# A linear-attention block and a gated spatial mixer in one program: denominators as one 1/den row per head, key weights loaded on ScalarE's queue, and a new order of all operations

## The chip, the cores and the metric

The program runs on one core of one Trainium2 chip. The metric is device time in microseconds (us) for one execution. A profile of one execution gives its span, from the first to the last instruction, and the trace that the later sections read.

## What is computed

Two blocks follow each other on x of 2048 tokens by 512 features (bf16). The first is a linear attention with 32 heads of 16 features, behind a layernorm and with a residual; the second is a gated mixer over the tokens, again behind a layernorm and with a residual. Cut to what matters:

```python
q, k, v = (layernorm(x) @ wqkv) split into 3 x 32 heads x 16
phi = lambda t: where(t > 0, t + 1, exp(t)) + 1e-06
pq, pk = phi(q), phi(k)
kv  = einsum('bhsd,bhse->bhde', pk, v)
z   = einsum('bhsd->bhd', pk)
num = einsum('bhqd,bhde->bhqe', pq, kv)
den = einsum('bhqd,bhd->bhq', pq, z)[..., None] + 1e-06
h   = x + (num / den) @ wo
zz  = gelu(layernorm(h) @ w_in);  z1, z2 = halves of 896 each
g   = w_sp @ layernorm(z2) + b_sp
h2  = h + (z1 * g) @ w_out
```

## The kernel before

**Stages.** The tokens are 16 tiles of 128 (NT) in 4 groups of 512 (NG, GW). In order of the data: layernorm of each x tile (DVE statistics, L571 and L575; 1/sqrt of the variance on ScalarE for tiles 0 to 3, on GpSimd for the others), transposition of the normalised tile (TensorE and a ScalarE copy, L640 and L647, for tiles 0 to 3; DMA transposes for the others), keys per tile (L729) and queries per group (L743), phi (Exp, Relu on ScalarE, L706 and L708, the rest on DVE), the product of pk with the normalised x (L761), the sum z (L773), a small chain that folds v and wo into one 512 x 512 matrix `mw` (L810, L828), the denominators (L843 to L874), attention plus residual (L893, L898), second layernorm, the two halves of the gelu layer (L925, L956), the mixing with `w_sp` (L995) and the last projection with its store (L1013, L1019, L1021).

**1/sqrt on ScalarE.** `rstd_act` (L584) is two activations on a 128 x 1 column: Ln of the variance (L585), then Exp of -1/2 times it (L587). Tiles 0 to 3 each have such a pair. ScalarE evaluates functions from a loaded table set. The kernel asks for one set by name, in a single operation of its own (L552), which no other operation is declared to depend on:

```python
op("act", 1.3, lambda e: e.preload_act_table_set("natural_log_exp_and_others"), bias=BIG - 1)
```

**Denominators before.** `den(gq)` works on one group of 512 tokens. Four matmuls (L843) multiply the columns `zb` (128 x 32 for each chunk c of 128 query features) with the queries; each writes its own 32 rows of one PSUM bank, so a row is a head of that chunk (eight heads, each repeated four times) and a column a token. ScalarE makes 1/den as exp(-ln(den)) on 128 x 512 (L848, L850). Four matmuls with 32 rows each (L858) spread the rows with the 0/1 matrix `sel` to the 128 feature rows of each chunk, into two tiles of two PSUM banks. One tile goes through a ScalarE copy to bf16 (L868) and a DVE product in SBUF (L870), the other straight into a DVE product with PSUM (L873). `den` is called once for each group.

**What sets the order.** `Program.op` only records operations with their reads and writes; from these come the semaphore waits. `Program.schedule` (L208) takes the order written out in `ORDER` (L15): a list of operation numbers, counted in the order in which the code records them. Each engine runs its own operations in that order, strictly one after the other. `SLOT` (L53) gives each temporary tile its PSUM bank or buffer. The costs and `LAG` are a planner's figures; no time on the chip follows from them.

On ScalarE the order before begins: the table load L552; Ln x0, Ln x1, Exp x0, Exp x1, Ln x2, Exp x2; the copies of transposed tiles 0, 1, 2; Ln x3, Exp x3; the copy of tile 3; then phi of the keys and of the queries of group 0. On SP it begins: loads of x tiles 0, 1, 2; the key weights `wk` (512 KB); x tile 3; the query weights `wq`; x tiles 4 to 15. On TensorE it begins: 8 matmuls on constants (L559), which give nothing to the result, three more of them behind DVE and ScalarE steps of tile 0, the transpositions of tiles 0, 1 and 2 with four short constant matmuls between and behind them, the keys of tiles 0 and 2, the transposition of tile 3, the keys of tile 1, and the first query chunk of group 0 (L743), which needs all four transposed tiles.

**The end.** The last tile is projected in two column ranges, 384 and 128 wide. Each is added to the residual by DVE and stored by a DMA that SP issues.

Of the kernel before, what the change touches and what calls it, by code (L numbers as in the profile page):

```python
# [5 lines left out]
FP32 = mybir.dt.float32  # L6
# [4 lines left out]
P = 128  # L11
# [48 lines left out]
]  # L60


# [1029 lines left out]
```

## Time and profile before

| | |
|---|---|
| median of 3 runs | 242.62 us (242.61 to 242.78) |
| span of the profiled execution | 241.1 us |
| TensorE busy | 236.2 us, 98% of the span |
| DVE busy | 135.3 us |
| ScalarE busy | 84.3 us |
| granted TensorE clock | 1.000 |

The profile gives the profiled execution's span; 1.5 us of the median (242.62 - 241.1) lie outside it. A row of the trace's timeline has the start in us, the busy us, the engine, the line, the operation, its output and input, how many instructions, and in brackets how long the engine had stood idle before and what ended that. PE is the matmul part of TensorE, PEld its weight loads, which run beside matmuls; ACT is ScalarE, POOL GpSimd, SP the engine whose queue issues most DMAs. A row of the chain of work that ended last has start, duration and the line, with the number of instructions.

### The profile page before, as it was taken

Reading aid. Unit: us, or ns where it says so; the run is one execution under the profiler, and the core shown is the slowest. Engines: PE = TensorE matmul, PEld = TensorE weight load, DVE = VectorE, ACT = ScalarE, POOL = GpSimd, SP = SyncE. Lnnn points to the kernel's source line nnn. Section 1 sums busy time; section 2 is a strip of 40 time slices with the busy share of each in tenths; the row PEclk is TensorE's granted clock in tenths of the full one; section 3 lists DMA queues with packets and bytes.
Section 4 is the critical chain, followed back from the end, with each engine's and each line's share of the span. In section 5 each row is a group of like instructions: output and inputs, shape, how many; then the busy total and the mean of one; then the engine's idle time right before and its main releaser. Section 6 shows DMA issues by size and latency. Waiting matters only on the chain.

```text
span 241.1 us, 2991 instructions
## 1 busy us (share of the span) xinstructions
PE 236.2 (98%) x1143; PEld 107.6 (45%) x1166; DVE 135.3 (56%) x269; ACT 84.3 (35%) x105; POOL 33.9 (14%) x87
## 2 busy tenths in 40 slices
PE   8999999999999999999999999999999999999995
PEld 2544443434444444445444444444444444444442
DVE  4899944699999986725833233342333423332443
ACT  4695744997776998455510000000000000000000
POOL 5123412002224472201300000000000000000000
PEclk9999999999999999999999999999999999999999
DMA  6933349954304343874544454430000100000022
GB/s 179 343 65 69 64 88 312 290 118 89 75 15 128 69 90 82 226 128 93 104 90 107 93 98 96 109 109 24 0 0 0 65 24 0 0 0 3 0 87 87
DMA packets 56702, 21.83 MB, mean 91 GB/s; under 512 B 50704, under 2 KB 55824, under 8 KB 56688
## 3 DMA queue, kind: packets, MB, share of 16 engines
q1 hardware_dynamic: 55744, 17.32, 32.4%
q0 software_dynamic: 944, 4.33, 5.3%
q8 instruction: 9, 0.15, 0.2%
q14 instruction: 5, 0.04, 0.1%
HBM read 7.47 MB, written 2.10 MB: 40 GB/s over the span
## 4 chain that ended last, share of the span: by engine, by line
PE 98%; issue 1%; DVEq 0%; DVE 0%
PE ps L995 40%; PE ps L925 10%; PE ps L956 10%; PE ps L1013 10%; PE ps L893 6%; PE ps L743 6%; PE ps L729 6%; PE ps L761 6%; PE ps L559 2%; PE ps L858 1%; PE ps L843 1%; PE ps L640 0%; PE ps L773 0%; PE ps L828 0%; PE ps L810 0%
## 5 line engine op out<-in xcount | busy, mean ns | idle before, releaser
L995 PE MATMUL ps<-wsp,pk_xn_z 128*128 128x512 bf16 x330 | 73.5, 379 | 0.3
L1002 DVE TENSOR_TENSOR e<-ps,e 128x512 bf16<-128x512 f32 x28 | 19.4, 692 | 64.0 <-PE ps L995 64.0
L995 PEld LDWEIGHTS ps<-wsp,pk_xn_z 128*128 128x128 bf16 x336 | 32.9, 98 | 39.4
L956 PE MATMUL ps<-hT,win 128*128 128x512 bf16 x110 | 26.4, 379 | 0.1
L925 PE MATMUL ps<-win,hT 128*128 128x384 bf16 (+1 forms) x124 | 26.0, 352 | 0.2
L1013 PE MATMUL ps<-wout,xT_pq_z 128*128 128x512 bf16 (+2 forms) x117 | 24.6, 366 | 0.1
L995 PE MATMUL ps<-wqkv_wsp,pk_xn_z 128*128 128x512 bf16 x109 | 24.2, 379 | 0.2
L934 DVE BATCH_NORM_STATS2 small<-pk_xn_z 128x6 f32<-128x512 bf16 (+1 forms) x32 | 18.4, 612 | 10.1 <-ACT pk_xn_z L930 10.0
L571 DVE BATCH_NORM_STATS2 small<-xh 128x6 f32<-128x512 bf16 x32 | 21.0, 675 | 3.3 <-DMA xh<-in_A_x_dram 3.2
L706 ACT ACTIVATE e<-ps 128x1024 bf16<-128x1024 f32 x16 | 16.5, 1032 | 9.7 <-PE ps L729 6.3
L961 ACT ACTIVATE xT_pq_z<-ps 128x1024 bf16<-128x1024 f32 (+1 forms) x16 | 14.5, 914 | 11.5 <-PE ps L956 11.5
L925 PEld LDWEIGHTS ps<-win,hT 128*128 128x128 bf16 x128 | 12.4, 98 | 12.6 <-issue 0.2
L1019 DVE TENSOR_TENSOR e<-ps,xh 128x512 bf16<-128x512 f32 (+2 forms) x17 | 11.1, 659 | 11.4 <-PE ps L1013 11.4
L1013 PEld LDWEIGHTS ps<-wout,xT_pq_z 128*128 128x128 bf16 x119 | 11.4, 98 | 13.1
L995 PEld LDWEIGHTS ps<-wqkv_wsp,pk_xn_z 128*128 128x128 bf16 x112 | 11.0, 98 | 13.2
L956 PEld LDWEIGHTS ps<-hT,win 128*128 128x128 bf16 x112 | 11.0, 98 | 12.6
L592 POOL TENSOR_TENSOR small<-small 128x2 f32<-128x2 f32 x22 | 16.4, 745 | 1.2
L930 ACT ACTIVATE pk_xn_z<-ps 128x896 bf16<-128x896 f32 x16 | 14.5, 914 | 5.3 <-PE ps L925 5.1
L743 PE MATMUL ps<-xT_pq_z,wqkv_wsp 128*128 128x512 bf16 x61 | 15.2, 380 | 0.3 <-issue 0.2
L729 PE MATMUL ps<-wqkv_wsp,xT_pq_z 128*128 128x512 bf16 x62 | 15.3, 379 | 0.1
L761 PE MATMUL ps<-pk_xn_z 128*128 128x512 bf16 x63 | 15.2, 379 | 0.2 <-issue 0.2
L590 POOL TENSOR_SCALAR small<-small 128x2 f32<-128x2 f32 x22 | 6.2, 280 | 63.2 <-DVE small L575 62.8
(72 smaller groups left out, 187.7 us busy)
## 6 DMA issues: line engine op xcount, KB each, us to landing
out_dram<-e SPq DMA_DIRECT2D x15, 128.0 KB, 1.7
win<-in_B_w_in_dram POOLq DMA_DIRECT2D x1, 1792.0 KB, 8.6
wqkv_wsp<-in_A_wqkv_dram SPq DMA_DIRECT2D x2, 512.0 KB, 4.5
xh<-in_A_x_dram SPq DMA_DIRECT2D x4, 256.0 KB, 5.5
wout<-in_B_w_out_dram POOLq DMA_DIRECT2D x1, 896.0 KB, 6.1
wsp<-in_B_w_sp_dram SPq DMA_TRANSPOSE x48, 2.9
xh<-in_A_x_dram SPq DMA_DIRECT2D x4, 128.0 KB, 2.5
xh<-in_A_x_dram SPq DMA_DIRECT2D x1, 512.0 KB, 6.8
```

The lines of the kernel that those rows point to most:

```text
L571: op("dve", dve_c(512), lambda e: e.bn_stats(s6.ap(), src.ap()), r=[src], w=[s6])
L592: return op("pool", 0.7, lambda e: e.tensor_tensor(dst.ap(), dst.ap(), h.ap(), ALU.pow), r=[dst, h], w=[dst])
L706: op("act", act_c(n), lambda e: e.activation(lo.ap(), t(flat).ap(), ACT.Exp), r=[t()], w=[lo])
L729: i = e.matmul(t(bank(ti)).ap(), lhsT=lhs.ap()[:, c, :], rhs=rhs.ap()[:, c, :], start=(c == 0), stop=(c == KD - 1))
L743: r_ = e.matmul(t(bank(i)).ap(), lhsT=lhs.ap()[:, c, :], rhs=rhs.ap()[:, c, :], start=(c == 0), stop=(c == KD - 1))
L761: r = e.matmul(txk[h](bank(i)).ap(), lhsT=xx.ap()[:, c * P:(c + 1) * P], rhs=kk.ap(), start=(n == 0), stop=(n == NT - 1))
L925: k = e.matmul(t(bank(i)).ap()[:, 0:b - a], lhsT=l.ap()[:, c, :], rhs=win[c, a:b].ap(), start=(c == 0), stop=(c == KD - 1))
L934: op("dve", dve_c(b - a), lambda e, s6=s6, src=src: e.bn_stats(s6.ap(), src.ap()), r=[src], w=[s6])
L956: k = e.matmul(t(bank(i)).ap(), lhsT=l.ap()[:, c, :], rhs=r_.ap()[:, c, :], start=(c == 0), stop=(c == KD - 1))
L995: k = e.matmul(t(bank(0)).ap(), lhsT=l.ap()[:, s - a, :], rhs=r_.ap()[:, s - a, :], start=(s == 0), stop=(s == NT - 1))
L1002: op("dve", dve_c(512), lambda e: e.tensor_tensor(gb().ap(), t(bank(0)).ap(), bsp().ap()[:, tg * GW:(tg + 1) * GW], ALU.add), r=[t(), bsp( ...
L1013: k = e.matmul(t(bank(0)).ap()[:, 0:b - a], lhsT=l.ap()[:, fc, :], rhs=wout[fc, a:b].ap(), start=(fc == 0), stop=(fc == KF - 1))
```

## The change

It has these parts.

1. **Denominators.** The query features are no longer taken in chunks of 128 neighbours but with a step of 4 (`f + i:D:KD`), so that each of the 32 heads has 4 rows in every chunk. The four chunks then add up in one row per head: `den(gs)` takes two groups of 512 tokens at once, with 16 matmuls of 128 x 32 by 256 columns that accumulate over c into four blocks of 32 rows, one block for each 128 tokens of a group. Ln and Exp are on 128 x 256, for two groups together. Four matmuls of 128 x 128 by 128 columns spread the rows of a group into one PSUM bank; ScalarE copies it to bf16 (128 x 512), and two DVE products in SBUF, each over half of the group's tokens with the row repeated for the four chunks, finish. `mw` is made by 16 matmuls of 32 output rows instead of 4 of 128.
2. **Loads.** `wk` is issued first on ScalarE's queue, beside SP's x0 to x3.
3. **Last tile.** The column ranges are 352 and 160; the second range's store is issued by ScalarE.
4. **Constant matmuls.** 9 at the start instead of 8; 3 later ones instead of 7.
5. **Order.** `ORDER` and `SLOT` are new for all operations. The planner's figures change too, without another effect.

```diff
 ORDER = [
-    29, 15, 0, 30, 18, 17, 21, 1, 16, 22, 31, 2, 13, 23, 32, 14, 3, 24, 33, 11, 4, 25, 34, 12, 5, 35, 38, 26, 6, 36,
...
+    27, 18, 21, 22, 28, 0, 13, 29, 30, 31, 32, 33, 34, 35, 24, 1, 15, 11, 12, 14, 36, 37, 38, 39, 2, 43, 44, 3, 4, 5,
...
+    86, 87, 106, 88, 143, 89, 148, 134, 97, 149, 90, 142, 83, 95, 91, 98, 150, 155, 156, 99, 26, 144, 104, 92, 100,
...
-    WARM = 8
+    WARM = 9
...
-    VIA_ACT = ((0, 0), (1, 0), (2, 0), (3, 0))
+    DEN = ((0, 1), (2, 3))
...
+    load("act", "wk", wqkv[:, D:2 * D], w3[:, :, D:2 * D], D * D * 2)
     load_x("sp", 0, 1)
     load_x("sp", 1, 2)
     load_x("sp", 2, 3)
-    load("sp", "wk", wqkv[:, D:2 * D], w3[:, :, D:2 * D], D * D * 2 + 50000)
     load_x("sp", 3, 4)
...
-    for gate, n, cost, count in ((first[0], 512, 2 * MM, 2), (rs_op[0], 512, 2 * MM, 1), (tr_op[0], 256, MM, 2),
-                                 (tr_op[1], 256, MM / 2, 2)):
+    for gate, n, cost, count in ((tr_op[0], 256, MM, 2), (tr_op[1], 256, MM / 2, 1)):
...
-            lhs = wqkv[:, (f + i) * P:(f + i + 1) * P]
+            lhs = wqkv[:, f + i:D:KD]
...
-                i = e.matmul(tzT(bank(0)).ap()[:, c * CG:(c + 1) * CG], lhsT=zr_v.ap[:, c * P:(c + 1) * P], rhs=part.ap,
+                i = e.matmul(tzT(bank(0)).ap()[:, c * CG:(c + 1) * CG], lhsT=zr_v.ap[:, c:D:KD], rhs=part.ap,
...
+        def mwmm(e, t=t, b=b):
+            for i in range(2):
+                for c in range(KD):
+                    k = e.matmul(t(bank(i)).ap()[CG * c:CG * (c + 1), :],
+                                 lhsT=kvT.ap()[:, c * P + 2 * b + i:(c + 1) * P:KD], rhs=wo[c, :].ap(),
+                                 start=True, stop=True, skip_group_check=True)
...
-    def den(gq):
+    def den(gs):
+        n = len(gs)
         t = Tile(PS)
-        r_ = pqT[gq].all()
+        pq = View(s_tq, (NG + gs[0]) * GB_, [n, KD, GW], BF16)
 
         def mm(e):
             for c in range(KD):
-                i = e.matmul(t(bank(0)).ap()[CG * c:CG * (c + 1), :], lhsT=zb.ap[:, CG * c:CG * (c + 1)],
-                             rhs=r_.ap()[:, c, :], start=True, stop=True)
+                for j in range(TPG):
+                    o = t(bank(0)).ap()[CG * j:CG * (j + 1), 0:n * P].rearrange("p (g k) -> p g k", g=n)
+                    i = e.matmul(o, lhsT=zb.ap[:, CG * c:CG * (c + 1)], rhs=pq.ap[:, :, c, j * P:(j + 1) * P],
+                                 start=(c == 0), stop=(c == KD - 1), skip_group_check=True)
             return i
...
+        op("act", act_c(n * P, 1), lambda e: e.activation(
+            flat(rr.ap()), t(bank(0)).ap()[:, 0:n * P], ACT.Ln, bias=eps[1:2].ap(), scale=1.0),
+           r=[t(), eps[1:2]], w=[rr])
+        last_lnexp.append(op("act", act_c(n * P), lambda e: e.activation(rb.ap(), rr.ap(), ACT.Exp, scale=-1.0),
+                             r=[rr], w=[rb]))
+        for gq in gs:
...
+                for j in range(TPG):
+                    k = e.matmul(t2(bank(0)).ap()[:, j * P:(j + 1) * P], lhsT=sel.ap[:, j * P:(j + 1) * P], rhs=r1.ap(),
+                                 start=True, stop=True, skip_group_check=True)
+                return k
+            op("pe", 4 * MS, sp_, r=[sel.all(), r1], w=[t2()])
+            op("act", act_c(GW), lambda e, t2=t2, rs=rs: e.activation(rs.ap(), t2(bank(0)).ap(), ACT.Copy), r=[t2()],
+               w=[rs])
+            for a in (0, GW // 2):
+                d, m = pqT[gq][:, a:a + GW // 2], rs_v[gq, a:a + GW // 2]
+                op("dve", dve_c(KD * GW // 2, 2), lambda e, d=d, m=m: e.tensor_tensor(
+                    d.ap(), d.ap(), m.ap().rearrange("p (a f) -> p a f", a=1).to_broadcast([P, KD, GW // 2]),
+                    ALU.mult), r=[d, m], w=[d])
...
-            op("sp", 0.5, lambda e, a=a, b=b, o_=o_: e.dma_start(out_dram[n * P:(n + 1) * P, a:b],
+            op("act" if a else "sp", 0.5, lambda e, a=a, b=b, o_=o_: e.dma_start(out_dram[n * P:(n + 1) * P, a:b],
...
-        project(n, [(0, D)] if n < NT - 1 else [(0, D - P), (D - P, D)])
+        project(n, [(0, D)] if n < NT - 1 else [(0, 352), (352, D)])
```

Counted through, the numbers of the new `ORDER` give these beginnings. The operation of L552 is number 26 (0 is the load of `wk`, 1 to 10 are SP's loads, 11 to 25 GpSimd's constants); ScalarE runs: the DMA of `wk`; Ln x0, Exp x0, Ln x1, Exp x1; copy of tile 0; Ln x2, Exp x2; copy of tile 1; Ln x3, Exp x3; copies of tiles 2 and 3; Exp of key pair 0; Exp, Relu of key pair 1; Exp, Relu of two query chunk pairs of group 0; Exp of key pair 2; **then number 26, the table load**; Exp of key pair 3 and so on. TensorE runs: 9 constant matmuls, transposition of tile 0, 2 constant ones, tile 1, 1 constant one, keys of tile 0, transposition of tile 2, keys of tile 1, transposition of tile 3, keys of tile 2, then the first query chunk of group 0. Further on, on TensorE, the denominators of groups 0 and 1 stand together in one place and those of groups 2 and 3 in another, and the two halves of the `mw` matmuls are neighbours. DVE's begin: statistics and aggregate of x0, of x1, normalisation of x0, statistics of x2, normalisation of x1, aggregate of x2, statistics of x3, normalisation of x2, aggregate of x3, statistics of x4, normalisation of x3.

More of the change, by code (lines that the diff above doesn't have):

```diff
@@ L154 @@
     __slots__ = ("eng", "fn", "cost", "prio", "deps", "after", "tiles", "seq", "start", "end", "pos", "sem",
-                 "semval", "marked", "clock", "lag", "bytes", "grp", "raw", "bias", "land", "late")
+                 "semval", "marked", "clock", "lag", "bytes", "grp", "raw", "bias", "land", "late", "mode")
 class Program:
     ENGINES = ("pe", "act", "dve", "pool", "sp")
-    LAG = {"pe": 0.17, "act": 0.12, "dve": 0.09, "pool": 0.1, "sp": 0.0}
+    LAG = {"pe": 0.163, "act": 0.1, "dve": 0.083, "pool": 0.045, "sp": 0.0}
     HOP = 0.06
@@ L170, in __init__, with op @@
         self.bias, self.late = 0.0, False
-    def op(self, eng, cost, fn, r=(), w=(), bias=0.0, after=(), dma=None, nbytes=0, land=2.0, lag=None):
+    def op(self, eng, cost, fn, r=(), w=(), bias=0.0, after=(), dma=None, nbytes=0, land=2.0, lag=None,
+           mode=0):
         o = Op()
@@ L175, in op @@
         o.bias, o.land, lag = bias + self.bias, land, self.LAG[eng] if lag is None else lag
-        o.late, o.start = self.late, None
+        o.late, o.start, o.mode = self.late, None, mode
         o.after, o.deps, o.tiles = list(after), {}, []
@@ L440, in bass_sequential_preLN__linear_attn_block__mixer_gmlp__prompt_kernel @@
     zb = small([KD * CG], BF16)
-    sel = small([P], BF16)
     ones = small([CG], BF16)
@@ L519, in bass_sequential_preLN__linear_attn_block__mixer_gmlp__prompt_kernel @@
     load_x("sp", 12, 16)
-    for a, b in zip(g.ops, g.ops[1:]):
+    for a, b in zip(g.ops[1:], g.ops[2:]):
         b.after.append(a)
@@ L574, in aggr @@
         d, s = st_row[k:k + 2], st_row[0:k]
-        op("dve", 0.1, lambda e: e.bn_aggr(d.ap(), s.ap()), r=[s], w=[d])
+        op("dve", 0.092, lambda e: e.bn_aggr(d.ap(), s.ap()), r=[s], w=[d])
     class Row:
@@ L584, in rstd_act @@
     def rstd_act(var, dst, scale=1.0):
-        op("act", 0.25, lambda e: e.activation(dst.ap(), var.ap(), ACT.Ln, bias=eps[0:1].ap(), scale=scale),
+        op("act", 0.195, lambda e: e.activation(dst.ap(), var.ap(), ACT.Ln, bias=eps[0:1].ap(), scale=scale),
            r=[var, eps[0:1]], w=[dst])
-        return op("act", 0.11, lambda e: e.activation(dst.ap(), dst.ap(), ACT.Exp, scale=-0.5), r=[dst], w=[dst])
+        return op("act", 0.103, lambda e: e.activation(dst.ap(), dst.ap(), ACT.Exp, scale=-0.5), r=[dst], w=[dst])
     def rstd_pool(var, dst, n):
-        op("pool", 0.25, lambda e: e.tensor_scalar(dst.ap(), var.ap(), EPS_LN, None, op0=ALU.add), r=[var], w=[dst])
+        op("pool", 0.18, lambda e: e.tensor_scalar(dst.ap(), var.ap(), EPS_LN, None, op0=ALU.add), r=[var], w=[dst])
         h = nhalf[0:n]
-        return op("pool", 0.7, lambda e: e.tensor_tensor(dst.ap(), dst.ap(), h.ap(), ALU.pow), r=[dst, h], w=[dst])
+        return op("pool", 0.665, lambda e: e.tensor_tensor(dst.ap(), dst.ap(), h.ap(), ALU.pow), r=[dst, h], w=[dst])
     def stats_act(n):
@@ L775, in zsum @@
         return i
-    op("pe", 0.88, zsum, r=[pk.all(), ones.all()], w=[tz()], land=3.0)
+    op("pe", 4 * MM, zsum, r=[pk.all(), ones.all()], w=[tz()], mode=1)
     for f in (0, 2):
@@ L824, in bass_sequential_preLN__linear_attn_block__mixer_gmlp__prompt_kernel @@
         t = Tile(PS, 2)
-        for i in range(2):
-            c = 2 * b + i
-            r_ = wo[c, :]
-            op("pe", MM, lambda e, t=t, i=i, c=c, r_=r_: e.matmul(
-                t(bank(i)).ap(), lhsT=kvT.ap()[:, c * P:(c + 1) * P], rhs=r_.ap(), start=True, stop=True),
-               r=[kvT, r_], w=[t()])
+        def mwmm(e, t=t, b=b):
[5 more added lines that the diff above has]
+            return k
+        op("pe", 2 * MM, mwmm, r=[kvT, wo.all()], w=[t()], mode=1)
         d = mw[2 * b:2 * b + 2, :]
@@ L876, in bass_sequential_preLN__linear_attn_block__mixer_gmlp__prompt_kernel @@
-    for gq in range(NG):
-        g.bias = -QGROUP * gq
-        if gq:
-            for f in (0, 2):
-                q_proj(gq, f)
-        den(gq)
+                for j in range(TPG):
+                    o = t(bank(0)).ap()[CG * j:CG * (j + 1), 0:n * P].rearrange("p (g k) -> p g k", g=n)
+                    i = e.matmul(o, lhsT=zb.ap[:, CG * c:CG * (c + 1)], rhs=pq.ap[:, :, c, j * P:(j + 1) * P],
+                                 start=(c == 0), stop=(c == KD - 1), skip_group_check=True)
@@ new lines, in mm @@
+            return i
+        op("pe", n * MM, mm, r=[zb.all(), pq.all()], w=[t()], mode=1)
+        rr, rb = rr_v[gs[0]:gs[-1] + 1, :], rb_v[gs[0]:gs[-1] + 1, :]
+        op("act", act_c(n * P, 1), lambda e: e.activation(
[3 more added lines that the diff above has]
+                             r=[rr], w=[rb]))
@@ L883, in bass_sequential_preLN__linear_attn_block__mixer_gmlp__prompt_kernel @@
+    for gs in DEN:
+        for gq in gs:
+            g.bias = -QGROUP * gq
+            if gq:
+                for f in (0, 2):
+                    q_proj(gq, f)
+        den(gs)
     for gq in range(NG):
```

71 lines of the change are left out of this document (24 added, 47 removed), and 79 rows, old and new, of tables (ORDER, SLOT).

## The prediction

> **What bounds the kernel now.** I read the page's busy times first, then its chain of work, then the chain in order of time at both ends of the span.
>
> ```profile
> PE 236.2 (98%) x1143; PEld 107.6 (45%) x1166; DVE 135.3 (56%) x269; ACT 84.3 (35%) x105; POOL 33.9 (14%) x87
> PE 98%; issue 1%; DVEq 0%; DVE 0%
> ```
>
> ```profile
> 0.83 5.00 PE ps L559 x11
> 5.83 0.04 issue
> 5.87 0.49 PE ps L640 x4
> ...
> 9.29 0.86 PE ps L729 x4
> 10.15 0.86 PE ps L743 x4
> ...
> 236.31 1.75 PE ps L1013 x9
> 238.06 0.02 issue
> 238.08 0.04 DVE e L1019
> ```
>
> TensorE is the chain, from 0.83 us to 238.06 us without a hole worth naming. Its first 5.0 us are constant matmuls, so useful work begins at 5.87. Time can come or go in three ways only: useful work begins earlier or later, TensorE's own work changes, or the 3.04 us behind the last matmul (241.1 - 238.06) change. Work on other engines is worth nothing unless TensorE then stands still.
>
> The point to hold on to is 10.15: the first query matmul. It needs all four of the first x tiles transposed. These rows of the timeline show what it waits for:
>
> ```profile
> 0.79 1.28 ACT L552 ACT_TABLE_LOAD   x1 [0.79 <-PEq L1077]
> 2.84 0.69 DVE L571 BATCH_NORM_STATS2 small<-xh 128x6 f32<-128x512 bf16 x1 [2.84 <-DMA xh<-in_A_x_dram]
> 5.24 0.18 DVE L575 BATCH_NORM_AGGREGATE small<-small 128x2 f32<-128x6 f32 x1
> 7.84 0.31 ACT L585 ACTIVATE small<-small 128x1 f32<-128x1 f32 x1
> 8.18 0.20 ACT L587 ACTIVATE small<-small 128x1 f32<-128x1 f32 x1
> 8.42 0.41 DVE L606 TENSOR_SCALAR pk_xn_z<-xh,small 128x512 bf16<-128x512 bf16 x1 [0.87 <-ACT small L587]
> 9.32 0.60 ACT L647 ACTIVATE xT_pq_z<-ps 128x512 bf16<-128x512 bf16 x1 [0.94 <-PE ps L640]
> 9.97 0.55 PEld L743 LDWEIGHTS ps<-xT_pq_z,wqkv_wsp 128*128 128x128 bf16 x4 [0.32 <-ACT xT_pq_z L647]
> ```
>
> Ln of tile 3 ends at 8.15, Exp at 8.38, its normalisation at 8.83; the copy of the transposed tile runs from 9.32 to 9.92, and the query's weights load at 9.97. The chain through ScalarE has 0.18 us of slack (10.15 - 9.97). Whatever delays ScalarE in front of that copy delays everything.
>
> **The table load, the step that decides.** The only load of the set that holds both Ln and Exp is L552's. It ran first; now ScalarE does all four Ln/Exp pairs and the first key's Exp ahead of it. Does something load a table for them?
>
> ```profile
> 65.08 0.63 ACT L850 ACTIVATE wsp<-wsp 128x512 bf16<-128x512 f32 x1
> 65.73 1.28 ACT L930 ACT_TABLE_LOAD   x1
> 67.02 0.92 ACT L930 ACTIVATE pk_xn_z<-ps 128x896 bf16<-128x896 f32 x1
> ```
>
> L930 is the gelu and asks for no load. So the build puts a load ahead of an activation whose function the set in force lacks. It took 1.28 us, began 0.02 after the activation before it (65.71), and the gelu began as it ended. It did not wait for the gelu's matmuls, so a load whose ScalarE is idle is hidden.
>
> Which set is loaded for an Ln with none in force, no row shows. If it holds Exp too, one load does, hidden while x0 is under way: cost nothing. If the choice is made for the function at hand, Ln gets a set without Exp, Exp one without Ln, and eight loads come, ahead of every Ln and Exp; all but the first stand between activations that have waited. I take the second end: the load at L930 was decided at the function, and L552 names its set by a string with two functions in it, which a program needs only where naming a function would not give that set.
>
> The sum for ScalarE then, from Ln x0 to the end of Exp x3: 4 Ln at 0.30, 4 Exp at 0.20, 7 loads at 1.30 with their gaps, and the two copies that the order puts between (tiles 0 and 1) at 0.60: 1.2 + 0.8 + 9.1 + 1.2 = 12.3 us. Ln x0 can begin when x0's statistics (2.84 to 3.53) and aggregate (0.18) are done, some 3.75. I add 0.2 because the 512 KB of `wk` now travel with x0 instead of behind x2; the ends are 0 and 0.9, the distance of x1's statistics from x0's:
>
> ```profile
> 3.72 0.69 DVE L571 BATCH_NORM_STATS2 small<-xh 128x6 f32<-128x512 bf16 x1 [0.18 <-DMA xh<-in_A_x_dram]
> ```
>
> So Exp x3 ends at 3.95 + 12.3 = 16.25. From there before's rows repeat: 0.94 to the copy, 0.60 for it, 0.1 to the matmul: 17.9, say 18.0 for the query's matmul. The same three key tiles precede it in both orders. The shift is 18.0 - 10.15 = +7.85 us. The operations of DVE behind x3's normalisation, and so POOL and the DMA transposes of tiles 4 to 15 on SP, move with it; nothing overtakes. `wk` at the head of ScalarE's queue costs only issue time ahead of activations that wait for x0 anyway, and SP's later loads move up, for nothing while ScalarE is late. The four constant matmuls fewer save nothing either: TensorE will stand idle there.
>
> TensorE now idles in pieces between some 4.7, when nine constant matmuls are through, and 17.0, when the copy of tile 2 (16.25 + 0.60) lets its keys begin. Before's first 4 us show what it is worth after idleness:
>
> ```profile
> 4.20 0.15 PEld L559 LDWEIGHTS ps<-const-bfloat16-1.0 128*128 128x128 bf16 x1 [0.28 <-issue]
> 5.22 0.10 PEld L559 LDWEIGHTS ps<-const-bfloat16-1.0 128*128 128x128 bf16 x1 [0.88 <-ACT small L587]
> ```
>
> Constant matmuls of 512 columns ran at 0.43 us each (0.15 + 0.28 from load to load) until some time between 4.35 and 5.22, twice the later 0.216 (0.86 for 4), and weight loads took 0.15 instead of 0.10, while the granted clock read 1.000. So about 3.9 us of work went at half rate. If that returns, the work from 17.0 on loses 3.9 / 2 = 1.95 us, less about 0.1 for the keys of tile 2, which would otherwise have had a gap behind them: +1.85. The ends are 0 (it stays fast) and 3.9 (twice as long). I take 1.85, since the only row of a TensorE out of idleness is slow.
>
> The Trainium skill, in "TensorE: Matmul & The Clock Gate" (The HAM clock gate), has this as a clock that halves after about 3.4 us of idleness and returns after as much sustained work. The start of this trace agrees; whether pauses broken by short work count as idle, no run here shows.
>
> The explicit load, now behind the Exp of key pair 2, is 1.28 us more for ScalarE. In such a stretch of before it has room:
>
> ```profile
> 18.00:28.00 10.00, 9.95 (x47) 4.57 (x47) 10.00 (x27) 5.93 (x7) 4.65 (x7) 1.00 0.34 68
> ```
>
> ScalarE is busy 5.93 of 10 us while TensorE is dense, so I cost it at nothing; without that cover up to 1.28.
>
> **The denominators on TensorE.** Small operations cost more than their columns:
>
> ```profile
> 43.29 0.55 PE ps L843 x8
> ...
> 44.81 0.89 PE ps L810 x16
> ...
> 47.86 0.33 PE ps L858 x4
> 48.19 0.97 PE ps L743 x4
> 49.16 0.97 PE ps L828 x4
> 50.12 1.73 PE ps L743 x8
> ...
> 54.48 0.33 PE ps L843 x4
> 54.81 0.97 PE ps L893 x4
> ```
>
> Four matmuls of 32 columns or 32 rows run side by side in the time of one, 0.22, but entering such a shape costs 0.11 (0.33 - 0.22) and leaving it 0.11 (0.97 - 0.86). Before: L843 in three places, 0.55 + 2 x 0.33, plus three exits, 1.54; L858 in four, 4 x 0.44 = 1.76; `mw` 0.86 (its 0.11 is counted). Together 4.16. After: two places of 16 matmuls with 256 columns, 4 x 0.108 = 0.43 plus 0.22 each, 1.30; the spreads are full 128 x 128 shapes of 128 columns, 16 x 0.0557 (0.89 / 16, L810) = 0.89, with no change of shape; `mw` 0.86 + 0.22. Together 3.27. That is -0.89 us, if four column blocks with 256 columns run side by side as those with 512 do; if not, +2.6 (two places, each 1.3 more). Weights with a step of 4 elements are read by 64 query loads:
>
> ```profile
> L743 PEld LDWEIGHTS ps<-xT_pq_z,wqkv_wsp 128*128 128x128 bf16 x64 | 5.8, 98 | 7.9 <-issue 1.1 <-ACT xT_pq_z L647 0.3 <-ACT e L868 0.3
> ```
>
> A load of 98 ns lies under a matmul of 216; it must more than double before it costs. I take 0.
>
> On the other engines the denominators get cheaper, and that lies beside TensorE:
>
> ```profile
> L873 DVE TENSOR_TENSOR xT_pq_z<-xT_pq_z,ps 128x1024 bf16<-128x1024 bf16 x4 | 4.8, 1204 | 0.1
> L870 DVE TENSOR_TENSOR xT_pq_z<-xT_pq_z,e 128x1024 bf16<-128x1024 bf16 x4 | 2.7, 675 | 0.0
> ```
>
> DVE has eight products of the 675 kind (5.4) instead of 4.8 + 2.7. Should the repeated row push them to 1204, 4.2 us more lie on DVE near 50 us, and attention tile 2 could wait some 2 us for its half.
>
> **The end.** These rows are SP's last stores:
>
> ```profile
> 238.67 0.81 SPq L1021 DMA_DIRECT2D out_dram<-e  x2
> 239.04 0.43 SPq L1021 DMA_DIRECT2D out_dram<-e  x1
> 238.56 0.28 DVE L1019 TENSOR_TENSOR e<-ps,xh 128x128 bf16<-128x128 f32 x1
> ```
>
> The last DVE sum ends at 238.84; its store could go then and goes at 239.04, behind the other one. From ScalarE's own queue it gains 0.2, less about 0.03 for 32 more columns in DVE: -0.15.
>
> **Sum.** The time around the profiled span (242.62 - 241.1 = 1.5) I leave as it is, so the sum counts against the median: 242.62 + 7.85 + 1.85 - 0.89 - 0.15 = 251.3 us.
>
> **The rivals.**
> One set for all: the build loads the set with both functions at Ln x0, hidden, and L552's load finds its cover. Then x0's aggregate follows its statistics at once, and its normalisation waits for x1's (3.72 + 0.2 for `wk`, 0.69 and 0.18): 4.8 to 5.2, transposition at 5.3 instead of 5.87. x3, no longer behind `wk`, keeps pace, and of the constant matmuls between the transpositions one short one is gone (0.11, half of a 512 one's 0.216): some -0.6. With -0.89 and -0.15 the time is 241.0, faster than before. It decides at one place, the first Exp: no load there, no shift. For it speaks that one set does hold both; against it that the build must look ahead. The Trainium skill, "ScalarE: Activation LUTs" (Table sets), counts one load for ln followed by exp, since natural_log_exp_and_others has both; by that rule the time is this rival's.
>
> No slow clock: alternating loads, but the work at 9 to 17 us keeps TensorE fast: 251.3 - 1.85 = 249.5. A clock that stays slow twice as long: 253.3.
>
> Dearer loads: should a load also drain the engine, each of the seven costs more. The rows against it are the 0.02 ahead of L930's load. The Trainium skill, same page (What ACT_TABLE_LOAD costs), puts about 1.38 us of drain beside 1.28 us of load; by it the sum would be 7 x 1.38 = 9.7 higher, 261. The trace has 0.02 in place of 1.38.
>
> The denominators stall: products at 1204 or column blocks in turn put 2 to 2.6 us on any case: 253.5 with the loads, 243.3 without.
>
> **How the numbers follow.** Alternating loads as summed, with either clock: 0.82, of which most near 251.3. One set for all: 0.11 at 241.0 and 0.02 at 243.3 with stalling denominators. Dearer loads: 0.05. A change of 0.2% (0.5 us) is about what a measurement of this kernel can tell from none. Faster 0.11, the same 0.01, slower 0.88. The range takes x0's 0 to 0.9, the clock's 0 to 3.9 and part of the denominators' 2.6: 248.0 to 254.5 holds the first case nearly whole, 0.80.
>
> **What would show it.** On ScalarE between 2 and 17 us: eight table loads, one ahead of each Ln and Exp, and ten in all instead of two; the copy of tile 3 near 17.3; the first L743 matmul near 18; TensorE's busy share low up to 17 us; matmuls at 0.43 us from 17 to 21. Right on the denominators: L843's successor in two places, and the spreads at 0.22 with no 0.97 behind them. Two loads or three in the whole trace and a first L743 before 10.15 would make it wrong.

## The result and the profile after

The changed kernel takes 253.61 us (median of 4 runs, 253.21 to 253.72), the kernel before 242.67 beside it: a ratio of 1.0443, 95% interval 1.0431 to 1.0456. It is 10.9 us slower. The profiled execution took 253.65 us, with a span of 251.9 against 241.1.

The page of the changed kernel, busy times, then shares of the chain that ended last:

```profile
PE 238.9 (95%) x1169; PEld 111.1 (44%) x1191; DVE 133.6 (53%) x269; ACT 89.7 (36%) x109; POOL 32.7 (13%) x84
PE 88%; ACT 7%; DMA 3%; issue 1%; DVE 1%; ACTq 0%
```

TensorE held 98% of the chain before and holds 88% now; 7% is ScalarE, which had no share. The groups by line and shape say what ScalarE does there (count, busy us and mean ns, idle time before):

```profile
L584 ACT ACT_TABLE_LOAD x4 | 5.1, 1283 | 4.2 <-DVE small L574 4.2
L586 ACT ACT_TABLE_LOAD x4 | 5.1, 1283 | 0.1
L551 ACT ACT_TABLE_LOAD x1 | 1.3, 1283 | 0.0
L930 ACT ACT_TABLE_LOAD x1 | 1.3, 1283 | 0.0
```

Ten table loads instead of two. L584 is Ln, L586 Exp of the 1/sqrt pair, L551 the explicit request: lines stand one lower than before. ScalarE's timeline shows where they lie:

```profile
4.18 1.28 ACT L584 ACT_TABLE_LOAD   x1 [4.18 <-DVE small L574]
5.47 0.29 ACT L584 ACTIVATE small<-small 128x1 f32<-128x1 f32 x1
5.79 1.28 ACT L586 ACT_TABLE_LOAD   x1
...
29.42 1.28 ACT L551 ACT_TABLE_LOAD   x1
```

For 13.4 us (4.18 to 17.62) ScalarE swaps tables around operations of 0.2 to 0.6 us. The load that the kernel asks for comes at 29.42, when all of it is over. The chain in order of time shows what followed (start, us, line, count):

```profile
17.42 0.21 ACT small L586
...
18.13 0.61 PE ps L639 x4
18.73 1.71 PE ps L727 x4
20.44 1.43 PE ps L741 x4
21.87 0.86 PE ps L727 x4
```

The first query matmul begins at 20.44 instead of 10.15, and four key matmuls of the same size take 1.71 at 18.73 and 0.86 at 21.87. The windows (length, busy us and count of each engine, granted clock, DMA share, GB/s) show that TensorE ran at a reduced clock:

```profile
0.00:5.00 5.00, 3.85 (x9) 1.16 (x9) 0.88 (x2) 0.82 (x1) 1.92 (x13) 1.00 0.56 184
5.00:18.00 13.00, 5.88 (x23) 2.42 (x23) 4.39 (x12) 12.78 (x19) 0.00 (x0) 0.61 0.54 171
18.00:20.00 2.00, 1.87 (x8) 1.01 (x9) 1.99 (x6) 1.33 (x3) 0.48 (x3) 0.50 0.00 0
...
22.00:24.00 2.00, 1.95 (x10) 1.03 (x10) 1.08 (x1) 1.23 (x2) 0.69 (x1) 1.00 0.45 92
```

From 5 to 18 us TensorE was busy 5.88 of 13, and it went into the dense work behind it at half clock. Two of the four timed executions list a mean granted clock of 1.000 and are no faster (253.72 and 253.57 us). That does not show a fast TensorE in them: the record reads 1.00 from 0 to 5 us as well, over matmuls of 0.43 us, and rows exist of the profiled execution alone.

**Where the 10.8 us of span came from.** Query start +10.29 (20.44 - 10.15); that query at half clock +0.57 (1.43 - 0.86); denominators -0.8 (below); one wait for a DMA transpose +0.81; the end -0.29. That is 10.58; the other 0.2 I cannot assign. The wait is seen in TensorE's timeline, ahead of the gelu layer:

```profile
98.94 1.02 PE L925 MATMUL ps<-win,hT 128*128 128x512 bf16 x3 [0.81 <-DMA hT<-xn]
```

### The profile page after: what moved, and what is told of

Same layout as the page of the kernel before. It is cut to its first block, busy times and chain, and to the rows that moved or that the text cites. A ratio compares the mean times of both kernels' runs of the same rounds, so it can differ in the third digit from the quotient of the medians.

```text
span 251.9 us, 3038 instructions
## 1 busy us (share of the span) xinstructions
PE 238.9 (95%) x1169; PEld 111.1 (44%) x1191; DVE 133.6 (53%) x269; ACT 89.7 (36%) x109; POOL 32.7 (13%) x84
## 4 chain that ended last, share of the span: by engine, by line
PE 88%; ACT 7%; DMA 3%; issue 1%; DVE 1%; ACTq 0%
PE ps L995 38%; PE ps L1013 10%; PE ps L956 9%; PE ps L925 8%; PE ps L741 6%; PE ps L893 6%; PE ps L759 5%; PE ps L727 5%; ACT L586 2%; ACT L584 2%; DMA hT<-xn 2%; DMA xh<-in_A_x_dram 1%; ACT xT_pq_z L961 1%; ACT xn L612 1%; ACT small L584 0%
## 5 line engine op out<-in xcount | busy, mean ns | idle before, releaser
L995 PE MATMUL ps<-wsp,pk_xn_z 128*128 128x512 bf16 x328 | 72.6, 379 | 0.4
L956 PE MATMUL ps<-hT,win 128*128 128x512 bf16 x109 | 25.3, 379 | 0.2
L727 PE MATMUL ps<-wqkv_wsp,xT_pq_z 128*128 128x512 bf16 x63 | 18.7, 427 | 0.1
L759 PE MATMUL ps<-pk_xn_z 128*128 128x512 bf16 x63 | 16.3, 379 | 0.2 <-issue 0.2
L956 PEld LDWEIGHTS ps<-hT,win 128*128 128x128 bf16 x112 | 10.9, 98 | 12.5 <-ACT pk_xn_z L930 0.3
L741 PE MATMUL ps<-xT_pq_z,wqkv_wsp 128*128 128x512 bf16 x61 | 16.0, 391 | 0.2
L591 POOL TENSOR_TENSOR small<-small 128x2 f32<-128x2 f32 x22 | 15.4, 705 | 1.1
L893 PE MATMUL ps<-pk_xn_z,xT_pq_z 128*128 128x512 bf16 x63 | 14.4, 379 | 0.2 <-issue 0.2
```

Source lines behind the costliest of these rows:

```text
L727: i = e.matmul(t(bank(ti)).ap(), lhsT=lhs.ap()[:, c, :], rhs=rhs.ap()[:, c, :], start=(c == 0), stop=(c == KD - 1))
L741: r_ = e.matmul(t(bank(i)).ap(), lhsT=lhs.ap()[:, c, :], rhs=rhs.ap()[:, c, :], start=(c == 0), stop=(c == KD - 1))
L759: r = e.matmul(txk[h](bank(i)).ap(), lhsT=xx.ap()[:, c * P:(c + 1) * P], rhs=kk.ap(), start=(n == 0), stop=(n == NT - 1))
L893: i = e.matmul(t(bank(ti)).ap(), lhsT=l.ap()[:, c, :], rhs=mw[c, :].ap(), start=(c == 0), stop=(c == KD - 1))
L956: k = e.matmul(t(bank(i)).ap(), lhsT=l.ap()[:, c, :], rhs=r_.ap()[:, c, :], start=(c == 0), stop=(c == KD - 1))
L995: k = e.matmul(t(bank(0)).ap(), lhsT=l.ap()[:, s - a, :], rhs=r_.ap()[:, s - a, :], start=(s == 0), stop=(s == NT - 1))
```

## The experiments

In kernels other than the changed one a line number can be one to four higher. L727, the keys, is L728 or L731, L741, the queries, L742 or L745. Operation 26 of the changed order is the table load, 0 the load of `wk`, 1 to 4 the loads of x0 to x3. Each kernel was timed beside the kernel before on the same chip, so ratios are what to compare between experiments. Edits of the order are cut to the numbers that moved and their neighbours.

### The table load alone

e1 is the changed kernel with one number moved in its order:

```diff
-    27, 18, 21, 22, 28, 0, 13, 29, 30, 31,
+    27, 18, 21, 22, 28, 0, 26, 13, 29, 30, 31,
...
-    150, 155, 156, 99, 26, 144, 104, 92,
+    150, 155, 156, 99, 144, 104, 92,
```

> The changed kernel with operation 26, the load of the table set that holds Ln and Exp, moved up in the order to stand right behind the issue of wk on ScalarE; nothing else differs. Theory (the alternating table loads cost the time): the eight loads at L584 and L586 go, two loads are left in the trace, and the time falls by about 10 us. What is left of the front is then set by x1, which landed at 5.3 us beside wk instead of 3.7: from there DVE has 3.8 us of work in order up to x3's aggregate, so the first query matmul stands near 11.6 us and the time near 243.5 us (242.67 + 1.4 - 0.8 denominators - 0.3 end + 0.8 for a wait near 98 us). Rival (the loads only fill time that ScalarE would have waited anyway, and the loss sits in the new order or in wk beside x): above 250 us. Rival (wk beside x costs nothing without the loads): 241 us.

Measured: 244.72 us (243.76 to 245.51), ratio 1.0066 [1.0042, 1.0090]. One number gives back 8.9 us of 10.9, 9.1 by the ratios. The executions spread; the profiled one took 243.83, near the 243.5 expected, with its first query at 12.13 instead of 11.6. Two loads are left, in ScalarE's timeline the first of them early:

```profile
1.29 1.28 ACT L552 ACT_TABLE_LOAD   x1 [1.29 <-PEq L1078]
3.88 0.29 ACT L585 ACTIVATE small<-small 128x1 f32<-128x1 f32 x1 [1.31 <-DVE small L575]
```

With that set in force neither Ln nor Exp gets a load. But the kernel is still 1.6 us (0.66%) above before, so something else in the front is late. VectorE's timeline has it:

```profile
5.48 0.70 DVE L571 BATCH_NORM_STATS2 small<-xh 128x6 f32<-128x512 bf16 x1 [1.70 <-DMA xh<-in_A_x_dram]
```

x1's statistics begin at 5.48, against 3.72 in the kernel before: x1 travels beside the 512 KB of `wk`. Under the changed kernel's loads this was covered.

e2 does the converse: the kernel before, with its table load (its number 29) behind the Exp of key pair 2 and nothing else changed.

```diff
-    29, 15, 0, 30, 18, 17, 21, 1, 16, 22,
+    15, 0, 30, 18, 17, 21, 1, 16, 22,
...
-    91, 217, 154, 150, 116, 149, 92, 151,
+    91, 217, 154, 29, 150, 116, 149, 92, 151,
```

> The kernel before with one edit: its table load (operation 29) stands behind the Exp of key pair 2, as in the changed kernel. Theory: the build puts six loads in front of the Ln and Exp of tiles 0 to 3 (the order before has Ln x0, Ln x1, Exp x0, Exp x1, so two pairs share loads), the first one behind its wait; the first query matmul moves from 10.15 to about 18.9 us and TensorE runs at half its rate until some 21 us: 251.5 us, 250.5 to 253. Rival (the loss of the changed kernel belongs to its new order, loads and denominators): 242.7 us. Rival (the build loads one set for both functions): 242.7 to 244 us.

Measured: 250.15 us (250.09 to 250.62), ratio 1.0299 [1.0281, 1.0317], a little under the range that was expected: the first query begins at 17.95, not 18.9, and takes 0.86, so the half clock had ended with the four keys ahead of it (1.07). The groups by line:

```profile
L585 ACT ACT_TABLE_LOAD x3 | 3.8, 1283 | 4.4 <-DVE small L575 4.4
L587 ACT ACT_TABLE_LOAD x3 | 3.8, 1283 | 0.1
```

Six loads here, because the order before has Ln x0, Ln x1, Exp x0, Exp x1 and so needs three pairs, not four. The mechanism works in a kernel without any other part of the change. The theory that one load serves Ln and Exp falls with the changed kernel and with e2.

### The first of the eight loads

e11 asks for a set with Ln right behind the issue of `wk`; L551's load stays late.

```diff
+    def wk_ln(e):
+        i = e.dma_start(wqkv[:, D:2 * D].ap(), w3[:, :, D:2 * D])
+        e.preload_act_table_set("natural_log")
+        return i
```

> The changed kernel with a load of a set for Ln asked for right behind the issue of the key weights, ahead of the first Ln; L552's load stays where the change put it. In the changed kernel the first of eight loads began only when VectorE's aggregate of x0 was done, 4.18, and so was not hidden. If that load is simply 1.28 us of the front, Ln of x0 begins at 4.2 and the time is 1.28 lower: 252.3. If the front's TensorE gaps take it back (clock, x1's landing at 5.3), 253.0 to 253.6.

Measured: 252.27 us (251.07 to 252.80), ratio 1.0374 [1.0342, 1.0406], 0.7% below the changed kernel's ratio, 1.7 us with some 0.8 of uncertainty. ScalarE's timeline:

```profile
1.30 1.28 ACT L511 ACT_TABLE_LOAD   x1 [1.30 <-PEq L1081]
4.22 0.29 ACT L588 ACTIVATE small<-small 128x1 f32<-128x1 f32 x1 [1.64 <-DVE small L578]
...
6.05 1.28 ACT L588 ACT_TABLE_LOAD   x1
```

Ln x0 runs at 4.22, not 5.47, and the first query matmul at 19.19, 1.25 earlier. That the total agrees so well with the 252.3 expected is partly luck: in e11's rows the query takes 1.71 and the keys behind it 1.45, so the half clock lasts longer, and the 0.81 wait for a transposed tile is absent. The rows still show that the first load, left to the build, was fully exposed. Why it waited, the chain of the changed kernel shows:

```profile
3.91 0.20 DVE small L574
...
4.13 0.02 ACTq L346
...
4.18 1.28 ACT L584
```

L346 is a semaphore wait that stands as an instruction of its own. The first Ln reads the variance, which VectorE makes, and the constant `eps`, which GpSimd makes, so it has two waits; in the trace one is this instruction and the other rides on the Ln, and the load lies between them. e2's first Ln is the same (wait at 4.35, load at 4.40). The later Lns read an `eps` that is known to be there and have one wait, and no such instruction precedes their loads: the one at 6.05 began while its Ln's input was still to come, at 6.68.

### The half clock

e8 is the changed kernel with 42 constant matmuls more in TensorE's idle pieces before 18 us: 12 of 512 columns behind the ninth, 15 of 256 behind each of two later ones.

```diff
+        def mm(e):
+            for _ in range(times):
+                k = e.matmul(idle(bank(0)).ap()[:, 0:n], lhsT=row[:, 0:P], rhs=row, start=True, stop=True)
+            return k
...
-        warm = [keep_busy(512, 2 * MM + 0.4 * (i == 0), warm)]
+        warm = [keep_busy(512, 2 * MM + 0.4 * (i == 0), warm, times=13 if i == WARM - 1 else 1)]
...
+            keep_busy(n, cost, [], [gate] if gate.eng != "pe" else [], times=16 if (gate is tr_op[1] or i) else 1)
```

> The changed kernel with 42 more constant matmuls in the pieces in which TensorE idles at the start (12 of 512 columns behind the ninth, 30 of 256 behind two later ones); the eight table loads stay. Theory (after idleness TensorE runs at half its rate, and that lies on the path from 18 to 21.5 us): the granted clock reads 1.00 from 5 us on, the keys of tile 2 take 0.86 us instead of 1.71 and the query chunk 0.86 instead of 1.43, and the time falls by 1.4 to 1.6 us to 252.0 us. Rival (the clock does not follow the work, or the half rate is hidden behind ScalarE): 253.6 us.

Measured: 252.83 us (252.53 to 253.02), ratio 1.0400 [1.0383, 1.0418]. The chain:

```profile
18.46 0.86 PE ps L731 x4
19.32 0.88 PE ps L745 x4
...
22.41 4.43 DMA xT_pq_z<-pk_xn_z
```

The keys take 0.86 again and the query begins 1.76 after the end of Exp x3 (19.32 - 17.56, where Exp x3 ends in it), against 2.82 in the changed kernel (20.44 - 17.62). With the query's own 0.57 the half clock cost 1.06 + 0.57 = 1.6 us. The total fell by only 0.8 (1.0 by the ratios), where 1.4 to 1.6 was expected: at 26.89 TensorE had waited 1.08 us for the second DMA transpose, issued at 22.41, where the changed kernel, coming later, has no wait. These keys stand only 0.6 ahead of the changed kernel's (26.89 against 27.48); that e8's span is 1.1 shorter is also owed to the 0.81 wait, which its profile does not have. The price is shown; more than half of it cannot be collected here.

### The key weights' queue and what came behind it

e3 is e1 with `wk` on SP between x2 and x3, where the kernel before had it.

```diff
-    27, 18, 21, 22, 28, 0, 26, 13, 29,
+    27, 18, 21, 22, 28, 26, 13, 29,
...
-    2, 43, 44, 3, 4, 5,
+    2, 43, 44, 3, 0, 4, 5,
...
-    load("act", "wk", wqkv[:, D:2 * D], w3[:, :, D:2 * D], D * D * 2)
+    load("sp", "wk", wqkv[:, D:2 * D], w3[:, :, D:2 * D], D * D * 2)
```

> As e1_table_first, and wk is issued by SP between x2 and x3 again, where the kernel before has it. Theory (wk beside the x loads delays x1 and x2, which DVE takes in order): x1 lands at 3.7 us again, the first query matmul moves to about 9.9 us, and the time is 242.0 us, 1.5 us under e1_table_first. Rival (the sixteen DMA engines deliver wk and x0 to x3 by the same time in any order, and x3 is what counts): the same as e1_table_first within 0.3 us.

Measured: 243.53 us (242.90 to 244.53), ratio 1.0028 [1.0015, 1.0041], 1.2 us below e1, so the rival falls; the first query moved to 11.07, not to 9.9. x1's statistics begin at 3.81 without a wait. What is late next is again a load, in VectorE's timeline:

```profile
8.91 0.69 DVE L571 BATCH_NORM_STATS2 small<-xh 128x6 f32<-128x512 bf16 x1 [1.16 <-DMA xh<-in_A_x_dram]
9.52 0.40 DVE L606 TENSOR_SCALAR pk_xn_z<-xh,small 128x512 bf16<-128x512 bf16 x1
```

The new order has x4's statistics ahead of x3's normalisation (9.52), and VectorE waits 1.16 us for x4 with x3's work ready. e5 moves x4's statistics (64) behind that normalisation (61):

```diff
-    55, 49, 58, 64, 59, 128, 60, 61, 66,
+    55, 49, 58, 59, 128, 60, 61, 64, 66,
```

> As e3_table_first_wk_sp, and in the order DVE's statistics of x4 stand behind the normalisation of x3 instead of ahead of it. Theory (in e3 DVE waited 1.2 us for the load of x4 while x3's normalisation stood behind it): the first query matmul moves from 11.07 to about 9.9 us and the time to 242.3 us, under the kernel before by 0.2%: the denominators' 0.8 and the end's 0.3 less some 0.6 for TensorE's idle pieces at the start. Rival (the new order loses elsewhere too, so the front is not what is left): 243.0 us or more.

Measured: 242.65 us (242.35 to 243.50) against 242.91 for the kernel before beside it, ratio 0.9991 [0.9979, 1.0003]: level with it, 0.9 below e3. In the profile the first query stands at 10.49, where 9.9 was expected.

e9 and e10 are e5 with VectorE's order shifted further (x3's statistics behind x2's normalisation, x11's behind the first key product), and e10 with `wk` behind x3 as well.

```diff
-    52, 57, 48, 126, 53, 127, 54, 55, 49,
+    52, 48, 126, 53, 127, 54, 57, 55, 49,
...
-    75, 137, 96, 70, 77, 78, 79, 214, 72, 71, 73, 130, 207, 131, 138,
+    75, 137, 70, 77, 78, 79, 214, 72, 71, 73, 130, 207, 131, 96, 138,
```

```diff
-    2, 43, 44, 3, 0, 4, 5,
+    2, 43, 44, 3, 4, 0, 5,
```

> e5 with two of VectorE's operations moved: the statistics of x3 stand behind the normalisation of x2 instead of ahead of it, and those of x11 behind the first key's product. If VectorE's order is what delays the front in e5 (it waited for x3's load with x2's normalisation ready, and the first key's product came 0.24 us late for TensorE), the transposition of tile 2 comes earlier where x3 lands late, the 0.24 us go, and the time is 0.2 to 0.5 us below e5: 242.2. If the first query is set by x3's own landing, nothing moves: 242.6.

> e9 with the key weights behind x3 on SP's queue instead of behind x2. If 512 KB ahead of x3 are what makes x3 late, x3's statistics begin 0.5 us or more earlier and the first query near 10.2: 241.7, below both kernels. If the key weights are then late, the first key matmuls wait for them and the time is 243 or more.

Measured: e9 243.07 us (242.75 to 244.14), ratio 1.0002 [0.9987, 1.0017]; e10 243.19 us (242.70 to 244.72), ratio 1.0013 [0.9995, 1.0031]. Neither gains. In e10 the keys wait for `wk`, as feared, by TensorE's timeline:

```profile
7.55 1.02 PE L728 MATMUL ps<-wqkv_wsp,xT_pq_z 128*128 128x512 bf16 x4 [0.88 <-DMA wqkv_wsp<-in_A_wqkv_dram]
```

x3's statistics were to begin 0.5 earlier in e10 and begin at 7.04, against 6.98 in e9; in neither do they wait for the load. In e9's profile the first query comes at 10.06, 0.4 before e5's 10.49, but that is no gain of its order: e12 below begins with e5's order number for number and has 9.79, because x3's load let its statistics begin at 6.53 there and at 7.23 in e5. The landing of the loads differs by that much between single executions. e9's profiled execution has a wait for a transposed tile of the second block, 0.56 us; e5's has none. e12 tests whether that wait keeps e5's median up: it is e5 with one block of z1 (553) ahead of token tile 9 (478).

```diff
-    469, 437, 478, 389, 553, 479,
+    469, 437, 553, 478, 389, 479,
```

> e5 with one matmul group of the gelu layer moved on TensorE: the fifth block of z1 for the second token group goes ahead of token tile 9 instead of behind its first half. In the profiles of the changed kernel and of e9 TensorE stands still 0.81 and 0.56 us there, for the DMA transpose of tile 9, and in e5's it does not. If that stall comes in part of the executions and is what keeps e5's median level with the kernel before, the median falls by 0.2 to 0.5, to 242.3, and the executions lie closer together. If the spread has another source (when the loads of x land), the median stays at 242.6; if PSUM is not free for the moved block, it rises above 243.

Measured: 242.82 us (242.63 to 243.53) against 242.85 for the kernel before, ratio 1.0001 [0.9992, 1.0010]. Its profile has no such wait, as e5's had none, and the median is not lower. TensorE's timeline at the front:

```profile
9.79 1.04 PE L742 MATMUL ps<-xT_pq_z,wqkv_wsp 128*128 128x512 bf16 x4
...
14.65 0.61 PE L760 MATMUL ps<-pk_xn_z 128*128 128x512 bf16 x2 [0.37 <-DVE pk_xn_z L714]
```

The query begins 0.36 before the kernel before's 10.15, and TensorE then waits 0.37 for VectorE's first key product: what the front gains ahead of the query, the wait takes. The product does not hang on the query: e12's chain comes to it through VectorE, from the landing of an x load at 8.88, and it ends at 14.60, against 13.75 in the kernel before. No version that was run beats the kernel before.

### The last store and `mw`

e4 is e1, and e6 is e5, with the last store on SP:

```diff
-            op("act" if a else "sp", 0.5, lambda e, a=a, b=b, o_=o_: e.dma_start(out_dram[n * P:(n + 1) * P, a:b],
+            op("sp", 0.5, lambda e, a=a, b=b, o_=o_: e.dma_start(out_dram[n * P:(n + 1) * P, a:b],
```

> As e1_table_first, and SP issues the last store again. Theory (the store waits for the one before it on SP's queue): 0.2 to 0.3 us over e1_table_first. Rival (the new column split, not the queue, shortened the end): no difference beyond 0.1 us.

> As e5_x4_behind, and SP issues the last store again. Theory (a store waits for the one ahead of it on SP's queue): 0.2 to 0.3 us over e5_x4_behind, and the last store is issued 0.3 us after DVE's last sum instead of 0.03. Rival: no difference beyond 0.1 us.

Measured: e4 245.12 us (243.80 to 246.97), ratio 1.0088 [1.0058, 1.0118], overlapping e1's interval and so inconclusive: the front of both varies by more than the store is worth. e6 243.46 us (242.86 to 244.41), ratio 1.0016 [0.9998, 1.0034], 0.8 above e5 (0.2 to 0.3 was expected) with intervals that just overlap. The traces agree on the sign: from the end of the last VectorE sum to the end of the span it is 2.55 us in e6 (241.1 - 238.55), 2.6 in e4 (244.5 - 241.91) and 2.0 in e5 (241.2 - 239.18). With SP's queue the new column split ends even later than the old one (2.26 in the kernel before), so in the traces the queue shortens the end and the split does not.

e7 is e5 with a query chunk between the two halves of `mw`:

```diff
-    247, 226, 593, 594, 595, 229, 251, 252, 265, 227,
+    247, 593, 594, 595, 229, 251, 252, 265, 226, 227,
```

> As e5_x4_behind, and one query matmul group stands between the two halves of the mw matmuls, so that TensorE enters and leaves the shape with 32 output rows once more. Theory (each entry and each exit costs 0.11 us, which is what the denominators save): 0.2 us over e5_x4_behind, and the row of the group behind each half reads 0.97 instead of 0.86. Rival (the 0.11 is how the profile draws it, no time): no difference in time.

Measured: 244.13 us (243.58 to 245.27), ratio 1.0045 [1.0028, 1.0063], 1.5 above e5. The chain of e7 first, then that of e5:

```profile
51.59 0.56 PE ps L828 x8
52.15 0.98 PE ps L742 x4
53.13 0.59 PE ps L828 x8
...
53.74 1.02 ACT pk_xn_z L835
...
58.76 0.62 PE ps L848 x16
```

```profile
51.56 0.99 PE ps L828 x16
...
57.86 0.55 PE ps L848 x16
```

Two visits to the 32-row shape cost 0.56 + 0.59 and 0.12 for the exit between (0.98 - 0.86), 1.27, against 0.99 for one: the second visit costs 0.28. The rest of the 1.5 is no matter of shapes: `mw`'s ScalarE copy (L835) also came later, the chain goes over to ScalarE behind it, and the second denominators begin at 58.76 instead of 57.86. That 0.9 is most of the 1.0 by which the two profiled spans differ (242.2 and 241.2). As a measure of the shape the run's time is useless, its rows are not.

## Why the prediction was right

The forecast was 251.3, range 248.0 to 254.5; 253.61 lies within, 2.3 above the point. By its steps:

**What bounds.** The chain through ScalarE to the first query decided, with 0.18 us of slack before. Right.

**The table loads.** Eight, ten in all, each ahead of its function, then nothing more: right, and shown alone by e1 and e2. The rival "one set for all" fell. The Trainium skill, "ScalarE: Activation LUTs" (Table sets), counts one load for ln followed by exp; here that held only where the joint set was already in force (e1), and where it was not, the build loaded one set per function. The Trainium skill, same page (What ACT_TABLE_LOAD costs), has 1.28 us for the load, which agrees (1283 ns), and 1.38 us of drain, which these rows do not show: 0.02 us lie ahead of each load and the activation begins as it ends.

**"All but the first" exposed.** This step failed: 1.28 us. The row quoted for it was the gelu's, whose load did not wait for the gelu's inputs. Here the first load began at 4.18, released by VectorE like the Ln itself. e11 shows the price in its rows, 1.25. The first Ln has a second wait as an instruction of its own, and the load stood behind that; the gelu's row has none ahead of it, and one example was taken for a rule.

**ScalarE's sum**, Ln x0 to the end of Exp x3, 12.3: measured 5.47 to 17.62, 12.15. Right.

**The delay by `wk`.** For x0 0.2 was taken; its statistics began at 3.18 against 2.84, 0.34. The ends (0 and 0.9) held it. What the prediction mis-sized was x1, to which the rival "one set for all" gave the same 0.2: it came 1.6 later (5.32 against 3.72). Under eight loads that costs nothing; without them it is part of why e1 takes 244.7 and not that rival's 241.0: `wk` back on SP gave 1.2 (e3) and VectorE's order another 0.9 (e5). What keeps e5 1.6 above that rival is taken up at the end of this section.

**From Exp x3 to the query**, 1.75 at full clock: 1.76 in e8. Right.

**The half clock**, +1.85: 1.6, by e8 and the rows. Right in mechanism and nearly in size. Whether pauses broken by short work count as idle was left open; e11 shows that they do (last section). The granted clock read 0.50 from 18 to 20, where before's start had read 1.000 with matmuls at the same slow rate. The prediction had the loss start at 17.0 with the keys of tile 2; they stood behind the transposition of tile 3 and began at 18.73, which changed nothing, for both ran slow. The constant matmuls are three fewer in all (12 after 15), not four; no term of the sum uses them.

**The denominators**, -0.89. The chain of the changed kernel:

```profile
57.61 0.55 PE ps L847 x16
58.16 0.99 PE ps L741 x4
...
60.04 0.45 PE ps L863 x8
...
61.35 0.99 PE ps L827 x16
62.34 1.85 PE ps L741 x8
...
67.64 0.55 PE ps L847 x16
68.20 0.16 issue
68.35 1.67 PE ps L893 x7
```

Two places of 0.55 with exits of 0.13 (0.99 - 0.86) and 0.10 (0.16 + 1.67 - 1.73), two spreads of 0.45, `mw` 0.99 with an exit of 0.12: 3.34 against 4.16 before, -0.82. The four column blocks do run side by side: 16 matmuls of 256 columns in turn would take 1.73 (16 x 0.108). The VectorE products of the repeated row stayed fast, and the strided weights cost their loads 116 ns instead of 98 (114 in e5, where none of them ran at half clock), under matmuls of 216:

```profile
L741 PEld LDWEIGHTS ps<-xT_pq_z,wqkv_wsp 128*128 128x128 bf16 x64 | 7.2, 116 | 7.4 <-issue 1.7
L871 DVE TENSOR_TENSOR xT_pq_z<-xT_pq_z,wsp 128x1024 bf16<-128x1024 bf16 x8 | 5.3, 684 | 0.1
```

So the rival of stalling denominators fell. The explicit load (29.42) cost nothing; no wait of TensorE follows it.

**The end**, -0.15: -0.29. The last store goes 0.03 after the last sum, and from that sum to the end of the span it is 1.97 (251.9 - 249.93), against 2.26 (241.1 - 238.84):

```profile
249.12 0.81 DVE L1019 TENSOR_TENSOR e<-ps,xh 128x352 bf16<-128x352 f32 x2 [0.35 <-PE ps L1013]
249.96 0.36 ACTq L1021 DMA_DIRECT2D out_dram<-e  x1
```

**Not in the sum:** the 0.81 for a transposed tile of the second block. It appears in the profiled executions of the changed kernel, of e4 (0.8) and of e9 (0.56) and in no other; e12, in whose profile it is absent, is no faster than e5. So what it adds to the median is open.

Together: 1.28 for the first load, 0.81 for the transposed tile and 0.23 for x0 (ScalarE could begin at 4.18, where the sum had 3.95) are 2.32, less 0.15 on ScalarE's sum, 0.25 on the clock and 0.14 at the end, plus 0.07 on the denominators: 1.9 of the 2.3 us between forecast and median. Half of what remains is the 0.2 of span without an owner. The other half is a slip in the base: the 1.5 us that were said to lie outside the span came from setting the median, 242.62, beside the span of another execution, 241.1. Of the kernel before, executions of 242.62 us list spans of 240.9 (beside e12), so 1.7 lie outside, as in the changed kernel (253.65 - 251.9).

**Where the gains went.** The denominators (-0.8) and the end (-0.3) are real in the rows. They hardly show in the total of e5 or e12. Part of that is in the rows: the new order's front leaves TensorE waiting for VectorE's first key product (0.24 and 0.37), and the matmuls behind that wait take longer too, in e12's chain:

```profile
14.65 0.61 PE ps L760 x2
15.26 1.00 PE ps L728 x4
```

Two matmuls take 0.61 instead of 0.43, and four 1.00 instead of 0.86: a wait of 0.37 costs 0.69. That is a reading of rows; no run isolated it. Nor does it close the account: -0.36 at the query, +0.69, -0.8 and -0.3 would put e12's span 0.8 below that of the kernel before, and it is 0.2 below (240.9 against 241.1). Where the rest went is open.

## What to carry to other kernels

A table request by name is a dependency that no operand shows: when an order is rewritten, it must stay ahead of the first function that relies on it, and the count of table loads in the profile tells at once whether it did. Before pricing a new position for a load, look at which small transfer shares its path: 512 KB beside x delayed x1 by 1.6 us, though x0 hardly noticed. When a front is shortened, look at the second engine in line; here a gain ahead of the first query met a wait for VectorE 5 us later. And before crediting an edit with a shift of a few tenths of a microsecond in one profile, look at how far two profiles of the same order lie apart; here it was 0.7.

## What the runs showed of the hardware that was not expected

- A table load can begin ahead of the wait of its activation or behind it. In the changed kernel the first began at 4.18, released by VectorE; in e2 it was the same (4.40). Both times the activation had two waits, and one stood ahead of the load as an instruction of its own. In e11 the second Ln's load began at 6.05 with no such instruction ahead of it, while the aggregate that this Ln reads ran from 6.50 to 6.68.
- The granted clock is not a full account of a slow TensorE: it read 1.00 from 0 to 5 us while matmuls of 512 columns took 0.43, and 0.50 from 18 to 20 us with the same 0.43.
- Weights read with a step of 4 elements load in 114 ns (e5), against 98 for neighbours.
- Pauses broken by short work count as idle for the clock. In the changed kernel it fell between 7 and 9 us (0.70 there, 0.50 behind), after one unbroken pause of 3.11 us. In e11 it fell in the same stretch (0.82), although the longest pause so far was 2.20 us and 0.62 us of work lay behind it. In the changed kernel the 5.88 us of work scattered over 13 us did not bring it back, and the four query matmuls at 20.44 still took 1.43.
